# Sliding-window attention with the keys on the partitions, in quarters of TensorE's array, before a mixture of experts

## The chip, the cores and the metric

The kernel runs on one core of a Trainium2 chip. The metric is the device time of one execution in microseconds (us), lower is better. All data are 32-bit floats.

## What is computed

Attention over 8 batches, 8 heads, 576 positions, head dimension 64, with a bias that falls linearly with the distance (slope 2^-(h+1) for head h) and a window of 128 keys that ends at the query. Its rows feed a mixture of 8 experts, of which each row uses the one with the largest gate logit.

```python
scores = scale * np.matmul(q, k.transpose(0, 1, 3, 2))
scores = np.where((rel >= 0) & (rel < 128), scores - slopes * abs(rel), -1e9)
attn = np.exp(scores - scores.max(-1, keepdims=True))
attn = attn / (attn.sum(-1, keepdims=True) + 1e-09)
x = (attn @ v), laid out as (8 * 576, 512)
logits = x @ w_gate                       # (4608, 8)
expert = argmax(logits); gate_w = softmax(logits)[expert]
out = gate_w * (relu(x @ w1[expert]) @ w2[expert])   # 512 -> 1024 -> 512
```

## The kernel before

q and k come with heads and dimensions as rows and batches and positions as columns, so a pair of heads fills the 128 partitions, 64 each. v comes with tokens as rows. The tokens are cut into 36 tiles of 128; nine tiles are two batches.

*Attention* (lines 161 to 245) loops over the tiles. For each of four pairs of heads, the scores `sp` of 128 queries against 256 keys (the tile before and the tile itself) are two products with 64 rows of weights (L183), VectorE scales them and adds the bias (`sn`, L189) and finds the row minimum of the negated scores (`smin`, L198), ScalarE makes the exponentials `pr` and their sums (L201), TensorE transposes them (`pt`, L208), VectorE or ScalarE evicts them (`pT`, L211, L213), and TensorE multiplies them with v (`at`, L217): the transposed probabilities are the weights, 64 columns of v stream. Per tile, VectorE divides by the sums (`x`, L225), TensorE turns the rows (`xt`, L230) for the gate's logits (`lg`, L235), and the row, times its gate weight, is written to `x_rows` in DRAM (L245).

*Routing* (L254 to L343) finds each token's slot and each slot's token, with a one-hot product on TensorE (`tok`, L335). *The experts* (L350 on) gather 128 rows at a time by index (`xg`), turn them (`tp`, L363), multiply with w1 (`hps`, L373) and w2 (`zp`, L386) and scatter the rows to the output (L392). Five tiles per expert are always there, two further tiles are unrolled, and more lie in a loop that these inputs don't enter.

A scheduler orders the instructions of each engine and sets all semaphores. Loads and row writes share SP's DMA queue, indirect ones GpSimd's.

Of the kernel before, what the change touches and what calls it, by code (L numbers as in the profile page):

```python
# [15 lines left out]
P = 128  # L16
MASKED = 1.0e9


@with_exitstack  # L20
def kernel(
    ctx: ExitStack,
    tc: tile.TileContext,
    qT: bass.AP,  # (H*D, B*S), rows (head, dim), columns (batch, position)
    kT: bass.AP,  # the same
    v: bass.AP,  # (B*S, H*D)
    moe_w_gate: bass.AP,  # (Dm, E)
    moe_w1: bass.AP,  # (E, Dm, F)
    moe_w2: bass.AP,  # (E, F, Dm)
    out: bass.AP,  # (B*S, Dm)  # L30
# [27 lines left out]
    consts = ctx.enter_context(tc.tile_pool(name="consts", bufs=1))  # L58
    rte = ctx.enter_context(tc.tile_pool(name="rte", bufs=1))
    w_pool = ctx.enter_context(tc.tile_pool(name="weights", bufs=2))  # L60

    ident = consts.tile([P, P], F32, name="ident")
    make_identity(nc, ident[:])

    # routing constants
    lt_strict = consts.tile([P, P], F32, name="lt_strict")
# [4 lines left out]
    ones_sq = consts.tile([P, P], F32, name="ones_sq")  # L71
    nc.gpsimd.memset(ones_sq[:], 1.0)
    zero_e = consts.tile([P, E], F32, name="zero_e")
    nc.gpsimd.memset(zero_e[:], 0.0)
    keep = consts.tile([P, E, NT], F32, name="keep")
# [3 lines left out]
    def iota(name, shape, pattern, base, mult):  # L79
        t_i = consts.tile(shape, I32, name=name + "_i")  # L80
        t_f = consts.tile(shape, F32, name=name)
# [12 lines left out]
    # the gate's weights, negated: the logits are kept negated  # L94
    wgn = rte.tile([P, DB, E], F32, name="wgn")
# [3 lines left out]
    lgn = rte.tile([P, NT, E], F32, name="lgn")  # L99
    lmin = rte.tile([P, NT], F32, name="lmin")  # L100

    # attention's rows, times their gate weight (positive, so it passes through the expert)
    x_d = nc.dram_tensor("x_rows", (N, Dm), F32, kind="Internal").ap()

    def load_weights(w1_src, w2_src):
        w1 = w_pool.tile([P, DB, F], F32, name="w1")
        w2 = w_pool.tile([P, FB, Dm], F32, name="w2")
# [7 lines left out]
    with tc.tile_pool(name="bias", bufs=1) as b_pool, \  # L115
         tc.tile_pool(name="ld", bufs=3) as ld, \
         tc.tile_pool(name="kld", bufs=2) as kld, \
         tc.tile_pool(name="soft", bufs=4) as soft, \
         tc.tile_pool(name="rows", bufs=2) as rows, \
         tc.tile_pool(name="ps_s", bufs=3, space=PSUM) as ps_s, \  # L120
         tc.tile_pool(name="ps_t", bufs=2, space=PSUM) as ps_t, \
         tc.tile_pool(name="ps_1", bufs=1, space=PSUM) as ps_1:
# [3 lines left out]
        rel_i = b_pool.tile([P, 2 * P], I32, name="rel_i")  # L126
        nc.gpsimd.iota(rel_i[:], pattern=[[-1, 2 * P]], base=P, channel_multiplier=1)
        rel = b_pool.tile([P, 2 * P], F32, name="rel")
        nc.gpsimd.tensor_copy(rel[:], rel_i[:])
        nbias = b_pool.tile([P, H, 2 * P], F32, name="nbias")  # L130
# [6 lines left out]
        nc.gpsimd.affine_select(  # keys 128 or more before the query  # L137
# [11 lines left out]
        def load(c):  # L149
            pair = c * CH // TP  # L150
            if c * CH % TP == 0:
                k_sb[pair] = kld.tile([P, HP, TP * P], F32, name="k_sb")
            q_sb[c] = ld.tile([P, HP, CH * P], F32, name="q_sb")
            v_sb[c] = ld.tile([P, CH, Dm], F32, name="v_sb")
# [6 lines left out]
        for t in range(NT):  # L161
# [9 lines left out]
            c0 = P if j == 0 else 0  # a pair's first tile has no tile before  # L171
            q0 = t % CH * P

            at = ps_1.tile([P, H, D], F32, name="at")
            ssum = rows.tile([P, H], F32, name="ssum")
            # two heads at a time that lie on the same partitions, so that a PSUM bank has one row tile's products
            for g in range(HP):
# [3 lines left out]
                sp = ps_s.tile([P, 2, 2 * P], F32, name="sp")  # L181
# [5 lines left out]
                # the scores, negated  # L187
                sn = soft.tile([P, 2, 2 * P], F32, name="sn")
# [4 lines left out]
                if j == mid:  # the second batch's queries see nothing of the first  # L193
                    nc.vector.memset(sn[HALF:, :, : P + HALF], MASKED)
# [283 lines left out]
```

## Time and profile before

| | |
|---|---|
| median of 2 runs | 1414.22 us (1411.57 to 1416.87) |
| the profiled execution, first to last instruction | 1414.8 us |
| TensorE products busy | 1371.2 us, 97% |
| VectorE, ScalarE, GpSimd busy | 354.4, 294.8, 99.0 us |
| attention's last `lmin` (L237) | at 766.37 us |

The span lies inside the interval of the runs and 0.6 us from their median, so no time of weight lies around it. A busy share is the time in which an engine has an instruction under way; a product that waits for its weights counts as busy. A row of the groups gives the source line, the engine, the operation, the tile written and those read, the shapes, the count, the busy time and the mean duration of one in ns.

### The profile page before, as it was taken

How to read it: one execution, taken by the hardware profiler on the slowest of the kernel's cores; microseconds unless marked ns; L12 is line 12 of the kernel's file. 1: busy time of each engine (PE TensorE's matmuls, PEld its weight loads, DVE VectorE, ACT ScalarE, POOL GpSimd, SP SyncE). 2: the span in 40 equal slices, each digit the busy share in tenths (PEclk: the TensorE clock that was granted, in tenths of full speed). 3: DMA queues.
4: the chain of work that ended last, by engine and by line, in shares of the span. 5: the costliest groups of instructions: out<-in, count | busy, mean ns of one | idle time of the engine just before them, and what ended most of it. 6: DMA issues, size and time to landing. Idle time of an engine off the chain costs nothing.

```text
span 1414.8 us, 12107 instructions
## 1 busy us (share of the span) xinstructions
PE 1371.2 (97%) x4708; PEld 918.1 (65%) x4708; DVE 354.4 (25%) x807; ACT 294.8 (21%) x907; POOL 99.0 (7%) x118
## 2 busy tenths in 40 slices
PE   7999999999999999999996799999999999999996
PEld 5667777777777677776765664647474747474654
DVE  3333333333333433333334410101010101010100
ACT  2322333233333223333322000000000000000000
POOL 2000000000000000000000502020202020101010
PEclk9999999999999999999999999999999999999998
DMA  7422131010211101100000223232323232222221
GB/s 283 142 89 97 38 120 38 28 45 32 83 59 38 53 8 60 38 16 15 8 16 16 83 69 107 78 107 82 108 79 109 76 110 79 80 72 83 78 88 48
DMA packets 45642, 100.96 MB, mean 71 GB/s; under 512 B 3727, under 2 KB 16015, under 8 KB 45584
## 3 DMA queue, kind: packets, MB, share of 16 engines
q1 hardware_dynamic: 38336, 79.70, 16.0%
q0 software_dynamic: 6720, 20.46, 4.2%
q8 instruction: 38, 0.62, 0.2%
q14 instruction: 20, 0.16, 0.0%
q10 hardware_dynamic: 528, 0.02, 0.0%
HBM read 81.28 MB, written 20.45 MB: 72 GB/s over the span
## 4 chain that ended last, share of the span: by engine, by line
PE 54%; issue 38%; POOL 6%; DVE 1%; POOLq 0%; ACT 0%; DVEq 0%; ACTq 0%
PE sp L183 19%; PE at L217 17%; PE pt L208 10%; PE lg L235 4%; POOL out_dram L392 3%; POOL xg L353 3%; PE xt L230 3%; PE tok L335 1%; POOL oh_c L327 0%; POOL nbias L137 0%; POOL nbias L133 0%; POOLq L392 0%; DVE oh_c L323 0%; DVE pre L263 0%; DVE x L225 0%
## 5 line engine op out<-in xcount | busy, mean ns | idle before, releaser
L183 PE MATMUL sp<-k_sb,q_sb 64*128 64x256 f32 (+1 forms) x576 | 290.3, 677 | 10.0 <-DMA k_sb<-in_kT_dram 7.8
L373 PE MATMUL hps<-xgT,w 128*128 128x320 f32 (+1 forms) x1152 | 292.6, 416 | 0.0
L386 PE MATMUL zp<-w,h_sb 128*128 128x512 f32 x672 | 292.4, 592 | 0.0
L217 PEld LDWEIGHTS at<-v_sb,pT 128*128 128x128 f32 x1088 | 243.6, 330 | 50.0 <-ACT pr L201 15.6
L373 PEld LDWEIGHTS hps<-xgT,w 128*128 128x128 f32 x1152 | 209.8, 191 | 84.5 <-issue 5.1
L217 PE MATMUL at<-v_sb,pT 128*128 128x64 f32 x1088 | 258.7, 422 | 1.1 <-ACT pT L213 0.7
L386 PEld LDWEIGHTS zp<-w,h_sb 128*128 128x128 f32 x672 | 125.8, 190 | 149.2 <-issue 149.2
L183 PEld LDWEIGHTS sp<-k_sb,q_sb 64*128 64x128 f32 x576 | 132.6, 312 | 78.6 <-issue 64.8
L208 PE MATMUL pt<-ident,pr 128*128 128x128 f32 x544 | 167.9, 432 | 0.0
L378 DVE TENSOR_SCALAR h_sb<-hps 128x320 f32<-128x320 f32 (+1 forms) x72 | 33.8, 469 | 488.0 <-PE hps L373 486.3
L201 ACT ACTIVATE pr<-sn,smin 128x256 f32<-128x256 f32 (+1 forms) x288 | 139.9, 488 | 66.0 <-DVE lmin L237 30.3
L208 PEld LDWEIGHTS pt<-ident,pr 128*128 128x128 f32 x544 | 104.1, 236 | 69.7 <-issue 52.1
L189 DVE SCALAR_TENSOR_TENSOR sn<-sp,nbias 128x512 f32<-128x512 f32 (+1 forms) x144 | 93.7, 653 | 98.9 <-PE sp L183 93.0
L213 ACT COPY pT<-pt 128x512 f32<-128x512 f32 (+1 forms) x72 | 40.4, 561 | 250.9 <-PE pt L208 250.9
L198 DVE TENSOR_REDUCE smin<-sn 128x2 f32<-128x512 f32 (+1 forms) x144 | 92.5, 645 | 0.4
L380 ACT ACTIVATE h_sb<-hps 128x320 f32<-128x320 f32 (+1 forms) x72 | 30.2, 419 | 298.8 <-PE hps L373 298.8
L391 ACT COPY zo<-zp 128x512 f32<-128x512 f32 x42 | 24.6, 585 | 282.2 <-PE zp L386 256.3
L211 DVE COPY pT<-pt 128x512 f32<-128x512 f32 (+1 forms) x72 | 47.5, 660 | 130.3 <-PE pt L208 130.3
L235 PEld LDWEIGHTS lg<-wgn,xT 128*128 128x128 f32 x288 | 65.3, 331 | 7.6 <-ACT pT L213 6.5
L235 PE MATMUL lg<-wgn,xT 128*128 128x8 f32 x288 | 65.3, 356 | 0.7 <-ACT xT L232 0.7
L327 POOL TENSOR_TENSOR oh_c<-oh_c,tokv 128x639 f32<-128x639 f32 x4 | 9.1, 2265 | 768.5 <-DVE oh_c L323 768.5
L392 POOL DMA_INDIRECT out_dram<-zo,s_idx x42 | 41.6, 990 | 263.9 <-ACT zo L391 249.4
(93 smaller groups left out, 436.8 us busy)
## 6 DMA issues: line engine op xcount, KB each, us to landing
w<-in_moe_w_dram SPq DMA_DIRECT2D x20, 2048.0 KB, 8.9
q_sb<-in_qT_dram SPq DMA_DIRECT2D x12, 768.0 KB, 4.7
k_sb<-in_kT_dram SPq DMA_DIRECT2D x12, 768.0 KB, 7.6
v_sb<-in_v_dram SPq DMA_DIRECT2D x12, 768.0 KB, 4.5
x_rows<-xs SPq DMA_DIRECT2D x36, 256.0 KB, 2.0
xg<-x_rows,g_idx POOLq DMA_INDIRECT x42
out_dram<-zo,s_idx POOLq DMA_INDIRECT x42
wgn<-in_moe_w_gate_dram ACTq DMA_DIRECT2D x1, 16.0 KB, 4.9
```

The source lines that it names most:

```text
L183: nc.tensor.matmul(sp[:, i, c0:], lhsT=q_sb[t // CH][part, h // 2, q0 : q0 + P], rhs=k_sb[pair][part, h // 2, (j - 1) * P + c0 : (j + 1) * ...
L189: nc.vector.scalar_tensor_tensor(sn[:, :, c0:], in0=sp[:, :, c0:], scalar=-(D ** -0.5), in1=nbias4[:, g // 2, :, half, c0:], op0=ALU.mult, ...
L198: nc.vector.tensor_reduce(smin[:], sn[:, :, c0:], axis=AX, op=ALU.min)
L201: nc.scalar.activation(pr[:, i, c0:], sn[:, i, c0:], AF.Exp, bias=smin[:, i : i + 1], scale=-1.0, accum_out=ssum[:, h : h + 1],)
L208: nc.tensor.transpose(pt[:, i, kb, :], pr[:, i, kb * P : (kb + 1) * P], ident[:])
L211: nc.vector.tensor_copy(pT[:, :, c0 // P :, :], pt[:, :, c0 // P :, :])
L217: nc.tensor.matmul(at[:, h, :], lhsT=pT[:, i, kb, :], rhs=v_sb[kt // CH][:, kt % CH, h * D : (h + 1) * D], start=(kb == c0 // P), stop=(kb ...
L230: nc.tensor.transpose(xt[:, db, :], xf[:, db * P : (db + 1) * P], ident[:])
L235: nc.tensor.matmul(lg[:], lhsT=xT[:, db, :], rhs=wgn[:, db, :], start=(db == 0), stop=(db == DB - 1))
L373: nc.tensor.matmul(hps[:, :step], lhsT=g["w"][0][:, db, fb * P : (fb + 1) * P], rhs=g["xT"][:, db, c : c + step], start=(db == 0), stop=(d ...
L386: nc.tensor.matmul(zp[:], lhsT=g["h"][:, fb, j * P : (j + 1) * P], rhs=g["w"][1][:, fb, :], start=(fb == 0), stop=(fb == FB - 1),)
L392: ins = nc.gpsimd.indirect_dma_start(out=out[:, :], out_offset=bass.IndirectOffsetOnAxis(ap=g["si"](j), axis=0), in_=zo[:], in_offset=None ...
```

## The change

The attention stage is written anew; the experts keep their code.

- A unit is two batches (`bp`) and two heads (`hp`), 16 in all. Scores are made transposed: 64 keys on the partitions, up to 192 queries on the columns. The two heads lie on the two halves of the array's rows, the two batches on the two halves of its columns, so four products use one quarter (64 x 64) each. `GR` packs nine key blocks (block, first column, queries) into four groups of `GC` = 384 columns; `KB` is 64 keys. The loop has 64 groups and makes scores two groups (`AHEAD`) before they are used.
- ScalarE takes the exponential of the scores without a shift, VectorE multiplies by `fac`, the exponential of bias and mask, which is made once. The result is already in the layout of the product with v, so nothing is transposed; v's blocks are the weights, also in quarters.
- The sums over keys are products on TensorE with a matrix of zeros and ones (`ind`), 32 columns of the array each, so four lie beside each other.
- Gate logits are made from rows that are not yet divided (`gate`, again in strips of 32 columns), turned (`turn`), divided and turned into gate weights per pair of batches (`scale`); `row` turns a tile of x and multiplies by both factors at the eviction. These steps are put behind the next units' work by a list (`tasks`), of which `some` does the next entry: three for the gate, `turn` and `scale`, then five for nine rows.
- The attention's instructions are kept in the order written (`tc.manual_schedule()`).
- Each sum is checked to lie in 1e-18 to 1e24; a flag goes through DRAM, and if it is set at the end, the kernel of before (`general_path`) runs and overwrites the output.
- Expert 0's weights are loaded during attention, expert 1's no longer; the routing's constants are made after attention instead of at the start.

```diff
+        GR = [[(0, 0, 192), (1, 192, 192)], [(2, 0, 192), (3, 192, 192)], [(4, 0, 192), (5, 192, 192)],
+              [(6, 0, 192), (7, 192, 128), (8, 320, 64)]]
+        QH = [(0, 5 * KB), (5 * KB, 4 * KB)]
...
+            qk = pool("qk", 3)
+            ep = pool("ep", 5)
+            ps_s = pool("ps_s", 2, space=PSUM)
+            ps_a = pool("ps_a", 1, space=PSUM)
+            ps_m = pool("ps_m", 2, space=PSUM)
...
+            for h in range(H):
+                sl = -(2.0 ** (-8.0 * (h + 1) / H))
+                for c0, n in ((0, 192), (192, 128), (320, 64)):
+                    nc.scalar.activation(fac[:, h, c0 : c0 + n], rel[:, :n], AF.Exp, scale=sl)
...
+            def scores(i):
+                u, g = divmod(i, 4)
+                sp = ps_s.tile([P, 2, 512], F32, name="sp")
+                for kb, c0, n in GR[g]:
+                    for c in range(2):
+                        for r in range(2):
+                            hs = slice(r * D, (r + 1) * D)
+                            nc.tensor.matmul(
+                                sp[c * KB : (c + 1) * KB, r, c0 : c0 + n],
+                                lhsT=k_sb[u][hs, c, kb * KB : (kb + 1) * KB],
+                                rhs=q_sb[u][hs, c, kb * KB : kb * KB + n], start=True, stop=True,
+                            )
+                pe = ep.tile([P, 2, GC], F32, name="pe")
+                nc.scalar.activation(pe[:], sp[:, :, :GC], AF.Exp, scale=SCALE)
...
+                    nc.vector.tensor_tensor(pe[:], pe[:], fac[:, h0 : h0 + 2, :], op=ALU.mult)
...
+            def values(u, half, kbs):
...
+                for kb in kbs:
+                    pe, c0, n = block(u, kb)
+                    lo, hi = max(q0, kb * KB), min(q0 + qn, kb * KB + n)
+                    for c in range(2):
+                        for r in range(2):
+                            nc.tensor.matmul(
+                                acc[r * D : (r + 1) * D, c, lo - q0 : hi - q0],
+                                lhsT=v_sb[bp][c * KB : (c + 1) * KB, kb, (2 * hp + r) * D : (2 * hp + r + 1) * D],
+                                rhs=pe[c * KB : (c + 1) * KB, r, c0 + lo - kb * KB : c0 + hi - kb * KB],
+                                start=(c, r) not in begun, stop=True, skip_group_check=True,
+                            )
...
+            def finish(u, half):
...
+                nc.scalar.copy(xT[bp][:, hp, : 2 * LQ].rearrange("p (b q) -> p b q", b=2)[:, :, q0 : q0 + n], acc[:, :, :n])
...
+                for par, lo, hi, pe, off in ops:
+                    for r in range(2):
+                        j = 2 * r + par
+                        nc.tensor.matmul(
+                            sm[32 * j : 32 * j + 32, lo - q0 : hi - q0],
+                            lhsT=none[:] if pe is None else ind[:, hp, :],
+                            rhs=fac[:, 0, :KB] if pe is None else pe[:, r, off + lo : off + hi],
+                            start=j not in begun, stop=True, skip_group_check=True,
+                        )
...
+            def gate(bp, c):
...
+                c0, n = ((0, LQ), (LQ, LQ), (2 * LQ, P))[c]
+                for hp in range(HP):
+                    nc.tensor.matmul(
+                        ps[32 * hp : 32 * hp + 32, :n], lhsT=wgd[:, hp, :], rhs=xT[bp][:, hp, c0 : c0 + n],
+                        start=True, stop=True,
+                    )
...
+            def row(bp, t):
+                ps = ps_m.tile([P, 512], F32, name="m")
+                for hp in range(HP):
+                    nc.tensor.transpose(ps[:, hp * P : (hp + 1) * P], xT[bp][:, hp, t * P : (t + 1) * P], ident[:])
+                xs = rows.tile([P, H, D], F32, name="xs")
+                nc.vector.tensor_tensor(
+                    xs[:], ps[:].rearrange("p (h d) -> p h d", h=H),
+                    rsg[bp][:, t, :].unsqueeze(2).to_broadcast([P, H, D]), op=ALU.mult,
+                )
...
+            for i in range(NG):
+                u, g = divmod(i, 4)
...
+                if i + AHEAD < NG:
+                    scores(i + AHEAD)
+                if g == 0:
+                    values(u, 0, (0, 1))
+                elif g == 1:
+                    values(u, 0, (2, 3))
+                elif g == 2:
+                    values(u, 0, (4,))
+                    finish(u, 0)
+                    some()
+                    values(u, 1, (3, 4, 5))
+                else:
+                    values(u, 1, (6, 7, 8))
+                    finish(u, 1)
+                    some()
+                    if hp == HP - 1:
+                        tasks.extend(behind(bp))
...
+        fl = fp.tile([1, 1], I32, name="fl")
+        nc.sync.dma_start(fl[:], flag_d[:, 0:1])
+        wrong = nc.values_load(fl[0:1, 0:1], min_val=0, max_val=1)
+    with tc.If(wrong > 0):
+        general_path(tc, qT, kT, v, moe_w_gate, moe_w1, moe_w2, out, S, H)
```

## Rows read from the trace of the kernel before

**Rows 1.** The page: busy us and share; the granted clock in 40 slices, in tenths.
```profile
PE 1371.2 (97%) x4708; PEld 918.1 (65%) x4708; DVE 354.4 (25%) x807; ACT 294.8 (21%) x907; POOL 99.0 (7%) x118
...
PEclk9999999999999999999999999999999999999998
```

**Rows 2.** Stretches: us, busy (count) of each engine, granted clock, DMA share, GB/s.
```profile
0.00:30.00 30.00, 20.00 (x66) 13.13 (x66) 12.18 (x31) 8.08 (x29) 8.03 (x30) 1.00 0.94 333
...
150.00:700.00 550.00, 550.00 (x1930) 397.70 (x1929) 198.53 (x475) 175.36 (x582) 0.00 (x0) 1.00 0.13 44
```

**Rows 3.** Attention's TensorE groups by form, whole run: busy us, mean ns.
```profile
L183 PE MATMUL sp<-k_sb,q_sb 64*128 64x256 f32 x512 | 273.5, 703 | 0.0
L217 PE MATMUL at<-v_sb,pT 128*128 128x64 f32 x1088 | 258.7, 422 | 1.1 <-ACT pT L213 0.7 <-DVE gw L241 0.4
...
L208 PE MATMUL pt<-ident,pr 128*128 128x128 f32 x544 | 167.9, 432 | 0.0
```

**Rows 4.** Timeline, 300 to 322 us: start, length, merged instructions, idle before.
```profile
306.25 2.08 PE L183 MATMUL sp<-k_sb,q_sb 64*128 64x256 f32 x6
...
313.35 2.07 PE L183 MATMUL sp<-k_sb,q_sb 64*128 64x256 f32 x4
...
317.68 0.50 PEld L183 LDWEIGHTS sp<-k_sb,q_sb 64*128 64x128 f32 x2 [0.33 <-issue]
317.68 1.22 PE L183 MATMUL sp<-k_sb,q_sb 64*128 64x256 f32 x2
```

**Rows 5.** Same shapes early and late: transposes by timeline, L373 by stretches.
```profile
308.26 1.11 PE L230 MATMUL xt<-ident,x 128*128 128x128 f32 x4
...
1382.19 0.60 PE L363 MATMUL tp<-ident,xg 128*128 128x128 f32 x4
...
807.95:810.06 2.11, 2.11 (x5) 1.36 (x6) 1.00 0.75 206
810.06:812.17 2.11, 2.11 (x9) 1.52 (x8) 1.00 0.72 223
```

**Rows 6.** The experts' products: groups by form, then the timeline at 1375 us.
```profile
L386 PE MATMUL zp<-w,h_sb 128*128 128x512 f32 x672 | 292.4, 592 | 0.0
L373 PE MATMUL hps<-xgT,w 128*128 128x320 f32 x1024 | 278.0, 433 | 0.0
...
1375.05 7.31 PE L373 MATMUL hps<-xgT,w 128*128 128x128 f32 x64
```

**Rows 7.** ScalarE's and VectorE's groups by form.
```profile
L201 ACT ACTIVATE pr<-sn,smin 128x256 f32<-128x256 f32 x256 | 127.4, 500 | 53.6 <-DVE lmin L237 30.3 <-DVE rsum L222 16.7 <-DVE smin L198 5.6
...
L189 DVE SCALAR_TENSOR_TENSOR sn<-sp,nbias 128x512 f32<-128x512 f32 x128 | 87.0, 682 | 83.3 <-PE sp L183 82.0 <-ACT pr L201 1.3
...
L213 ACT COPY pT<-pt 128x512 f32<-128x512 f32 x64 | 37.5, 585 | 236.5 <-PE pt L208 236.5
...
L225 DVE TENSOR_TENSOR x<-at,rsum 128x512 f32<-128x512 f32 x36 | 24.9, 692 | 108.9 <-PE at L217 108.9
...
L201 ACT ACTIVATE pr<-sn,smin 128x128 f32<-128x128 f32 x32 | 12.5, 392 | 12.4 <-DVE smin L198 12.4
...
L189 DVE SCALAR_TENSOR_TENSOR sn<-sp,nbias 128x256 f32<-128x256 f32 x16 | 6.6, 420 | 15.6 <-PE sp L183 10.9 <-POOL nbias L137 4.1 <-ACT pr L201 0.6
...
L213 ACT COPY pT<-pt 128x256 f32<-128x256 f32 x8 | 2.9, 364 | 14.4 <-PE pt L208 14.4
...
L82 POOL IOTA tokv_i<- 128x36 int32 x1 | 0.2, 153 | 0.0
```

**Rows 8.** The page: the instruction queue's packets and MB; a small load's landing.
```profile
q8 instruction: 38, 0.62, 0.2%
...
wgn<-in_moe_w_gate_dram ACTq DMA_DIRECT2D x1, 16.0 KB, 4.9
```

**Rows 9.** Timeline: the last tile's `lmin`, and the first `oh_c` of the routing.
```profile
766.37 0.16 DVE L237 TENSOR_REDUCE lmin<-lgn 128x1 f32<-128x8 f32 x1
...
776.74 0.82 DVE L323 TENSOR_TENSOR oh_c<-iota_r,rc 128x639 f32<-128x639 f32 x1
```

More of the change, by code (lines that the diff above doesn't have):

```diff
@@ L20, with general_path @@
 @with_exitstack
-def kernel(
+def general_path(
     ctx: ExitStack,
@@ L56 @@
     assert LC <= 512
[L58 to L62, printed above, removed]
+    consts = ctx.enter_context(tc.tile_pool(name="g_consts", bufs=1))
+    rte = ctx.enter_context(tc.tile_pool(name="g_rte", bufs=1))
+    w_pool = ctx.enter_context(tc.tile_pool(name="g_weights", bufs=2))
+    ident = consts.tile([P, P], F32, name="g_ident")
     make_identity(nc, ident[:])
-    lt_strict = consts.tile([P, P], F32, name="lt_strict")
+    lt_strict = consts.tile([P, P], F32, name="g_lt_strict")
     nc.gpsimd.memset(lt_strict[:], 1.0)
@@ L79, in iota @@
     def iota(name, shape, pattern, base, mult):
-        t_i = consts.tile(shape, I32, name=name + "_i")
-        t_f = consts.tile(shape, F32, name=name)
+        t_i = consts.tile(shape, I32, name="g_" + name + "_i")
+        t_f = consts.tile(shape, F32, name="g_" + name)
         nc.gpsimd.iota(t_i[:], pattern=pattern, base=base, channel_multiplier=mult)
@@ L112 @@
     expert_w = {}
[L115 to L126, printed above, removed]
+    with tc.tile_pool(name="g_bias", bufs=1) as b_pool, \
+         tc.tile_pool(name="g_ld", bufs=3) as ld, \
+         tc.tile_pool(name="g_kld", bufs=2) as kld, \
+         tc.tile_pool(name="g_soft", bufs=4) as soft, \
+         tc.tile_pool(name="g_rows", bufs=2) as rows, \
+         tc.tile_pool(name="g_ps_s", bufs=3, space=PSUM) as ps_s, \
+         tc.tile_pool(name="g_ps_t", bufs=2, space=PSUM) as ps_t, \
+         tc.tile_pool(name="g_ps_1", bufs=1, space=PSUM) as ps_1:
+        rel_i = b_pool.tile([P, 2 * P], I32, name="g_rel_i")
         nc.gpsimd.iota(rel_i[:], pattern=[[-1, 2 * P]], base=P, channel_multiplier=1)
-        rel = b_pool.tile([P, 2 * P], F32, name="rel")
+        rel = b_pool.tile([P, 2 * P], F32, name="g_rel")
         nc.gpsimd.tensor_copy(rel[:], rel_i[:])
-        nbias = b_pool.tile([P, H, 2 * P], F32, name="nbias")
+        nbias = b_pool.tile([P, H, 2 * P], F32, name="g_nbias")
         for h in range(H):
@@ L151, in load @@
             if c * CH % TP == 0:
-                k_sb[pair] = kld.tile([P, HP, TP * P], F32, name="k_sb")
-            q_sb[c] = ld.tile([P, HP, CH * P], F32, name="q_sb")
-            v_sb[c] = ld.tile([P, CH, Dm], F32, name="v_sb")
+                k_sb[pair] = kld.tile([P, HP, TP * P], F32, name="g_k_sb")
+            q_sb[c] = ld.tile([P, HP, CH * P], F32, name="g_q_sb")
+            v_sb[c] = ld.tile([P, CH, Dm], F32, name="g_v_sb")
             cols = slice(c * CH * P, (c + 1) * CH * P)
@@ L172 @@
             q0 = t % CH * P
-            at = ps_1.tile([P, H, D], F32, name="at")
-            ssum = rows.tile([P, H], F32, name="ssum")
+            at = ps_1.tile([P, H, D], F32, name="g_at")
+            ssum = rows.tile([P, H], F32, name="g_ssum")
             for g in range(HP):
@@ L186 @@
                     )
-                sn = soft.tile([P, 2, 2 * P], F32, name="sn")
+                sn = soft.tile([P, 2, 2 * P], F32, name="g_sn")
                 nc.vector.scalar_tensor_tensor(
@@ L204 @@
                     )
-                pt = ps_t.tile([P, 2, 2, P], F32, name="pt")
+                pt = ps_t.tile([P, 2, 2, P], F32, name="g_pt")
                 for i in range(2):
@@ L237 @@
             nc.vector.tensor_reduce(lmin[:, t : t + 1], lgn[:, t, :], axis=AX, op=ALU.min)
-            gex = rows.tile([P, E], F32, name="gex")
-            gw = rows.tile([P, 1], F32, name="gw")
+            gex = rows.tile([P, E], F32, name="g_gex")
+            gw = rows.tile([P, 1], F32, name="g_gw")
             nc.scalar.activation(gex[:], lgn[:, t, :], AF.Exp, bias=lmin[:, t : t + 1], scale=-1.0, accum_out=gw[:])
@@ L261 @@
         )
-        pre = sm.tile([P, E, NT], F32, name="pre")
+        pre = sm.tile([P, E, NT], F32, name="g_pre")
         nc.vector.tensor_tensor_scan(
@@ L291 @@
         )
-        xe_f = sm.tile([1, NX + 1], F32, name="xe_f")
+        xe_f = sm.tile([1, NX + 1], F32, name="g_xe_f")
         nc.vector.reduce_sum(xe_f[:, :NX], xk[:], axis=AX)
@@ L366, in layer1 @@
     def layer1(g):
-        g["h"] = wk_pool.tile([P, FB, NJ * P], F32, name="h_sb")
+        g["h"] = wk_pool.tile([P, FB, NJ * P], F32, name="g_h_sb")
         step = min(LC, g["n"] * P)
@@ L383, in layer2 @@
         for j in range(g["n"]):
-            zp = mps.tile([P, Dm], F32, name="zp")
+            zp = mps.tile([P, Dm], F32, name="g_zp")
             for fb in range(FB):
@@ L397, in layer2 @@
             if g["apart"]:
-                tc.declare_no_dep(ins, group="rows_out", reason="disjoint rows")
-                tc.add_to_no_dep_group("rows_out", ins)
+                tc.declare_no_dep(ins, group="g_rows_out", reason="disjoint rows")
+                tc.add_to_no_dep_group("g_rows_out", ins)
     def fetch(ex):
```

596 lines of the change are left out of this document (543 added, 53 removed).

## The prediction

> **What bounds the kernel now.** I read the page's busy shares first, then the stretches, then the groups by form, and last the order of single instructions. TensorE is busy 97% of the span [rows 1]. In the steady part of attention it is busy all of the 550 us, VectorE 199 and ScalarE 175 [rows 2]: attention is bound by TensorE, and what the other engines do is hidden. Attention ends at 766.4 us with the last tile's `lmin` [rows 9]; 648.4 us of the span of 1414.8 lie behind it (routing, experts, end). The median of the runs, 1414.2, is that span to within 0.6, so sums against the span need no correction.
>
> The groups say where those 766 us go [rows 3]: one scores product a head (273 us in the full form), 1088 weight loads and products against `v` (259), 544 transposes of the probabilities (168). Each f32 product is two instructions, a transpose one. The reader is to see that `at` streams only 64 columns for 128 loaded weights, and that the scores use 64 of the 128 rows.
>
> Two things decide what the same arithmetic costs in another shape. First, halves of the array do run together: four score instructions take 2.07 us, but six that lie on both halves take 2.08, where two take 1.22 [rows 4]. From four against two, one 256-column instruction costs (2.07 - 1.22) / 2 = 0.425 us: 1.66 ns a column. Second, the clock. Four 128x128 transposes take 1.11 us in attention and 0.60 in the last experts; the first 2.11 us of the first expert hold 5 products, the next 2.11 hold 9 [rows 5]. Full-speed products cost 292.4 / 672 = 0.435 us for 512 columns [rows 6]: 0.85 ns a column, half of 1.66. The granted clock reads full speed in both [rows 1]; against it I go by the durations: attention runs at the 1.2 GHz level throughout, the experts at 2.4.
>
> **The change part by part.** It removes the 544 probability transposes, their 144 evictions, the maxima and accumulator reads. A unit is two batches by two heads; there are 16. Its TensorE work, in columns times instructions:
> - scores: (7 x 192 + 128 + 64) = 1536 columns on each of four quarters, two instructions each: 12,288. At 1.66 ns 20.4 us one after another, 5.1 if four run at once;
> - values: the same 1536 columns a quarter, over 11 pieces: 20.4 or 5.1;
> - sums, moved from ScalarE's accumulator to TensorE: (2 x 1536 + 128) x 2 = 6,400: 10.6, or 2.7 with four strips of 32 columns at once;
> - gate, per pair of batches 4 x 1152 x 2 = 9,216: 15.3 or 3.8, a quarter of it per unit: 3.8 or 1.0;
> - 45 transposes per pair of batches at 0.213 us (128 columns at 1.66): 9.6, per unit 2.4;
> - changes of the array's shape, about six a unit: the scores' weight loads sat 0.33 us behind such a change [rows 4]. 2 us; ends 0 (overlapped) and 4.
>
> With all four quarters at once a unit is 5.1 + 5.1 + 2.7 + 1.0 + 2.4 + 2 = 18.3 us at the low level and about half, 9.2, at the high one; with no overlap 20.4 + 20.4 + 10.6 + 3.8 + 2.4 + 1 = 58.6 at the low one. Before, 766 / 16 = 48. Rows 4 show two row halves at once; column halves and strips they do not show, so the overlap lies between 1 and 4. I take 4: the two halves seen cost nothing extra, which is as near as a row comes.
>
> The other engines, per unit. ScalarE: four exponentials of 768 elements, 0.81 us by the copies' slope (585 against 364 ns for 512 and 256) or 0.93 by the exponentials' [rows 7], 3.5; evictions of 640, 384 and 128 elements 0.70 + 0.48 + 0.25; `turn` 0.36: 5.3. VectorE: four multiplies of 768 at 682 + 256 x 1.02 = 0.94 [rows 7], 3.8; two sums 0.49 + 0.42; per pair of batches the gate's adds 1.7, some 30 small operations of `scale` 6.3, nine rows at 0.69 = 6.2, a quarter of it 3.6: 8.3. So at the low clock TensorE has 18.3 against 8.3 and hides them; at the high clock 9.2 against 8.3, and nothing hides a wait: the multiply of two groups ahead queues on VectorE behind `scale`, whose operations wait for `turn`'s copies. Between 9.2 (perfect) and 17.5 (the two added up) I take 12, nearer the first as the loop runs two groups ahead. Loads: 1.18 MB of q and k, 0.59 of v, 0.59 of rows per unit; the first 30 us moved 333 GB/s [rows 2], so 7.1 us a unit: hidden, and the floor if all else shrinks. `x_rows` and loads share SP's queue, and a row's write waits for its multiply there; loads queued behind it are for two units later, so it holds nothing.
>
> The start: ScalarE makes `fac` in 24 exponentials of 64 to 192 columns ahead of the first real one. By the exponentials' slope they take about 0.25 to 0.3 each once the accumulator is gone, 7 us after some 3 of set-up: 10 us until TensorE can go on. The end: the last pair's gate, `scale` and nine rows have nothing left to hide them: 1.7 + 6.3 + 6.2 of VectorE, with transposes and copies between, 20 us (ends 14 and 30).
>
> Behind attention: first, GpSimd builds the constants after attention, 40 small iotas among them, some 10 us by its 0.15 us operations [rows 7], beside VectorE's 10 us from `lmin` to `oh_c` [rows 9]: 0 to 8, I take 3. Second, expert 1's weights, loaded during attention before, now load beside expert 0's gathers: 0 to 5, I take 3; they are wanted only an expert later. Third, the flag's load and branch at the end: a small load lands in 4.9 us [rows 8] and no work is left to cover it: 0 to 12, I take 5. Together +11. The experts' products don't change.
>
> **Sum.** At the high level: 10 + 16 x 12 + 8 (four times 2 us of `scale` in the way) + 20 = 230; 230 + 648.4 + 11 = 889 us. Against the span of 1414.8 a saving of 525.
>
> **A rule against the change.** In rows 6, products on the same rows come 0.27 us apart for 320 columns, which is the streaming alone: the next weights load under the running product. The Trainium skill ("TensorE: Matmul & The Clock Gate", section on packing small matmuls) says a weight load overlaps a running product only when its row group differs; rows 6 disagree, as all their products use all rows. If it held between column halves, the 160 score and value instructions a unit would each show their load: rival 3's 965 us by the rule, 889 by the rows.
>
> **The rivals.**
> 1. The clock stays at the low level, as in all of attention before, although TensorE never paused there. For it: the durations of rows 4 and 5 there; against it: the first expert's dense products raised it at once [rows 5], and the change takes out the short products and most transposes. 10 + 16 x 18.3 + 25 + 659 = 987. Two quarters at once with the high level gives about the same, since both halve the rate.
> 2. Only the row halves overlap, at the low level: 10.2 + 10.2 + 10.6 + 3.8 + 2.4 + 2 = 39 us a unit, 624 + 35 + 659 = 1318; with strips overlapping by two, 32 a unit and 1206.
> 3. Weight loads between column halves show: 64 weights are half of the 128 whose load sets `at`'s pace of 259 / 1088 = 0.238 [rows 3], so 0.12 us, 160 of them over two row halves 9.5 us a unit, halved at the high level: 889 + 76 = 965. This is the skill's rule above.
> 4. TensorE cannot be fed: 225 pairs of load and product a unit. The densest stretch shows 64 in 7.31 us, 0.114 each [rows 6], but it is set by its 128 columns. At that pace 25.7 us a unit: 411 + 35 + 659 = 1105. Against it: in rows 4, six came in the time of four. The instruction queue carried 0.62 MB in 38 packets over the whole run [rows 8]; attention's 3604 pairs alone now want three quarters of that in a fifth of the time.
> 5. Slower: the quarters don't overlap at all (a wait between tiles of one bank or shape): 58.6 x 16 + 35 + 659 = 1632. It decides below an overlap of about 1.4, where a unit costs 45 us.
> 6. The check fails and `general_path` runs behind it: 889 + 1414 = 2303. The row sums of weights near 1 in a window lie between 1 and 128, far inside 1e-18 to 1e24, so under 1%.
>
> **How the numbers follow.** Forecast (four at once, high level) 0.55; rivals 1 and 3, with a clock that changes between levels, 0.25 together; rival 4 0.05; rival 2 0.07; rivals 5 and 6 0.03; better than 840, down to loads' floor 10 + 16 x 7.1 + 20 + 659 = 803, 0.05. The forecast's own bounds: 840 (10 us a unit, small end terms) to 950 (15 a unit, large ones). The range takes in rivals 1 and 3 with it: 840 to 1020, about 0.8. Faster by over 2% (what a measurement of this kernel can tell) 0.96, within 2% 0.01, slower 0.03.
>
> **What would show it.** After: TensorE's instructions of `sp` four to a start time, a unit in 12 us, attention ending near 230; transposes of the rows at 0.105 us pitch (else rival 1); starts of the second column half held back to the end of the first (rivals 2, 3); TensorE idle with no releaser (rival 4). The forecast is wrong if VectorE's multiply turns out to be what TensorE waits for most, at over 14 us a unit, or if the clock falls back in the waits.

## The result and the profile after

The changed kernel takes 875.65 us, median of two runs (874.09 to 877.21), against 1414.22: a ratio of 0.619, 95% interval 0.6145 to 0.6229. Forecast were 889, with 840 to 1020 as the range. The profiled execution is the one of 877.21 us; its span is 875.4. Of the six executions of the version with both repairs below, one took 3822 us and the others 862 to 866; its median is over all six.

The page of the changed kernel: busy us and share, the granted clock in 40 slices, the instruction queue, and attention's groups with the idle time ahead of them (these rows answer to [rows 1, 3, 8]).
```profile
PE 790.2 (90%) x5674; PEld 510.1 (58%) x5674; DVE 207.1 (24%) x421; ACT 137.3 (16%) x267; POOL 97.7 (11%) x166
...
PEclk8899999988559999999999999999999999999997
...
q8 instruction: 47, 0.77, 0.4%
...
L654 PE MATMUL at<-pe,v_sb 64*64 64x192 f32 (+2 forms) x1408 | 65.1, 297 | 16.4 <-DVE pe L628 7.8
...
L619 PE MATMUL sp<-q_sb,k_sb 64*64 64x192 f32 (+2 forms) x1152 | 63.1, 338 | 8.4 <-DMA q_sb<-in_qT_dram 7.5
...
L625 ACT ACTIVATE pe<-sp 128x768 f32<-128x768 f32 x64 | 51.8, 810 | 97.1 <-PE sp L619 95.6
L628 DVE TENSOR_TENSOR pe<-pe,fac 128x768 f32<-128x768 f32 x48 | 45.9, 957 | 54.3 <-ACT pe L625 54.3
```
`sp` and `at` are now busy for 128 us where `sp`, `at` and the transposes took 700 [rows 3]. By the forecast's own count each streams 12,288 columns a unit: one after another at the high clock (0.85 ns a column, [rows 6]) 10.4 us a unit, 167 us each in all. The mean of one instruction (297 and 338 ns) says nothing here, since several run at once; the busy time of the group does.

The timeline shows the order of four groups in the steady part, TensorE alone (start, length, merged instructions).
```profile
119.16 0.83 PE L654 MATMUL at<-pe,v_sb 64*64 64x192 f32 x16
...
119.81 0.84 PE L619 MATMUL sp<-q_sb,k_sb 64*64 64x192 f32 x24
...
120.46 0.73 PE L654 MATMUL at<-pe,v_sb 64*64 64x192 f32 x16
...
121.01 0.83 PE L619 MATMUL sp<-q_sb,k_sb 64*64 64x192 f32 x16
```
The 24 instructions at 119.81 are three key blocks of 192, 128 and 64 columns, each on four quarters in two instructions: 384 x 8 = 3072 columns. One after another they would take 2.6 us; the next group starts 0.65 us later. That is the factor of four.

Now the stretches: one undisturbed unit, then a unit in which the gate's `scale` runs, cut in two (columns as in [rows 2]).
```profile
53.30:61.30 8.00, 7.51 (x218) 6.67 (x215) 3.98 (x6) 4.38 (x8) 0.00 (x0) 1.00 0.30 104
...
121.90:129.90 8.00, 6.00 (x129) 4.99 (x125) 6.59 (x27) 2.73 (x5) 0.00 (x0) 1.00 0.11 25
129.90:138.30 8.40, 5.54 (x104) 4.52 (x108) 4.89 (x12) 3.13 (x7) 0.00 (x0) 0.80 0.40 131
```
An undisturbed unit takes 8.0 us with TensorE busy 94%; this one holds scores, values and sums only, as the first pair's gate and rows come later. (For the unit's borders the start of every fourth exponential L625 is taken.) The unit with `scale` takes 16.4, TensorE is busy 11.5 of it, and the granted clock leaves 1.00 in the second half. What stands in the way is read from the timeline there:
```profile
125.47 0.65 DVE L740 TENSOR_TENSOR s<-gsr 128x8 f32<-128x8 f32 x6 [0.98 <-ACT gsr L730]
...
128.51 1.18 DVE L761 TENSOR_REDUCE logits<-pr 128x72 f32<-128x576 f32 x1
...
130.25 0.26 ACT L767 ACTIVATE ex<-ex 128x72 f32<-128x72 f32 x1 [4.64 <-DVE ex L764]
...
130.42 0.79 ACT L625 ACTIVATE pe<-sp 128x768 f32<-128x768 f32 x1
...
131.42 0.95 DVE L628 TENSOR_TENSOR pe<-pe,fac 128x768 f32<-128x768 f32 x1
...
132.28 0.42 DVE L698 TENSOR_TENSOR sumT<-m,sumT 128x256 f32<-128x256 f32 x1
...
132.76 1.11 PE L781 MATMUL m<-ident,xT 128*128 128x128 f32 x4 [4.13 <-DVE sumT L698]
```
TensorE stops for 4.13 us, and its row names what ended the stop: `sumT` (L698), which empties one of the two buffers `m`. It stands in VectorE's queue behind the whole chain of `scale`, which ends at 131.5, and behind the multiply of the next scores (L628). ScalarE's queue is held too: the gate's exponential `ex` (L767) stands in it ahead of the next scores' exponential (L625) and waits 4.64 us for the same chain. But that exponential is done at 131.21, before VectorE is free, so in this stop VectorE's chain comes last. The four transposes after it take 1.11 us, the low-clock figure of [rows 5]; at 87.94 us the same four take 0.66.

Another wait shows in the list of waits for 32 to 200 us (total us, times, the longest):
```profile
DVE xs L783 <- DMA x_rows<-xs: 14.3, 5, 5.5
```
VectorE's multiply of a row waits until an earlier row has been written out of its buffer.

The end of attention and the routing, by the timeline (they answer to [rows 9]), then the end of the span:
```profile
216.29 0.23 DVE L762 TENSOR_REDUCE lmax<-logits 128x9 f32<-128x72 f32 x1
...
229.57 0.82 DVE L974 TENSOR_TENSOR oh_c<-iota_r,rc 128x639 f32<-128x639 f32 x1
...
250.21 1.19 POOL L1007 DMA_INDIRECT xg<-x_rows,g_idx  x1 [7.13 <-DVE s_idx L996]
...
262.14 0.77 PE L1027 MATMUL hps<-xgT,w 128*128 128x320 f32 x2
...
858.67 0.30 SPq L1109 DMA_DIRECT2D fl<-flag  x1
859.45 0.98 POOL L1046 DMA_INDIRECT out_dram<-zo,s_idx  x1 [13.03 <-ACTq L1094]
```
Attention's gate ends at 216.3 where it ended at 766.4. From there to the end of the span are 659.1 us, before 648.4. The routing runs at the low level, as slices 11 and 12 of the clock row show: the granted clock is 0.50 from 214.4 us for 47.8 us.

### The profile page after: what moved, and what is told of

The parts are those of the page before. It is cut to its first block, busy times and chain, and to the rows that moved or that the text cites. A ratio compares the mean times of both kernels' runs of the same rounds, so it can differ in the third digit from the quotient of the medians.

```text
span 875.4 us, 12886 instructions
## 1 busy us (share of the span) xinstructions
PE 790.2 (90%) x5674; PEld 510.1 (58%) x5674; DVE 207.1 (24%) x421; ACT 137.3 (16%) x267; POOL 97.7 (11%) x166
## 4 chain that ended last, share of the span: by engine, by line
issue 62%; PE 13%; POOL 8%; DVE 6%; DMA 6%; ACT 1%; SPq 1%; POOLq 0%; DVEq 0%; ACTq 0%
POOL out_dram L1046 5%; PE sp L619 4%; POOL xg L1007 4%; PE at L654 4%; DMA x_rows<-xs 3%; PE tok L986 2%; DMA v_sb<-in_v_dram 2%; PE m L687 2%; PE m L707 1%; DMA xg<-x_rows,g_idx 1%; PE m L781 1%; DVE xs L783 1%; ACT pe L625 1%; DVE pe L628 1%; DVE pr L754 1%
## 5 line engine op out<-in xcount | busy, mean ns | idle before, releaser
L654 PE MATMUL at<-pe,v_sb 64*64 64x192 f32 (+2 forms) x1408 | 65.1, 297 | 16.4 <-DVE pe L628 7.8
L619 PE MATMUL sp<-q_sb,k_sb 64*64 64x192 f32 (+2 forms) x1152 | 63.1, 338 | 8.4 <-DMA q_sb<-in_qT_dram 7.5
L1007 POOL DMA_INDIRECT xg<-x_rows,g_idx x42 | 40.3, 960 | 271.5 <-PE tp L1017 254.3
L625 ACT ACTIVATE pe<-sp 128x768 f32<-128x768 f32 x64 | 51.8, 810 | 97.1 <-PE sp L619 95.6
L654 PEld LDWEIGHTS at<-pe,v_sb 64*64 64x64 f32 x1408 | 49.7, 142 | 27.9 <-DVE pe L628 9.4
L628 DVE TENSOR_TENSOR pe<-pe,fac 128x768 f32<-128x768 f32 x48 | 45.9, 957 | 54.3 <-ACT pe L625 54.3
L619 PEld LDWEIGHTS sp<-q_sb,k_sb 64*64 64x64 f32 x1152 | 45.8, 146 | 15.9 <-DMA k_sb<-in_kT_dram 4.5
L781 PE MATMUL m<-ident,xT 128*128 128x128 f32 x144 | 27.4, 327 | 20.8 <-DVE sumT L698 16.8
L1018 DVE COPY xgT<-tp 128x512 f32<-128x512 f32 x42 | 27.7, 688 | 53.4 <-PE tp L1017 53.4
L687 PE MATMUL m<-pe,ind 128*32 128x192 f32 (+2 forms) x704 | 30.9, 294 | 1.7 <-issue 1.7
L783 DVE TENSOR_TENSOR xs<-m,rsg 128x512 f32<-128x512 f32 x36 | 24.5, 685 | 17.3 <-DMA x_rows<-xs 14.3
```

Of the source, the lines that this page charges most:

```text
L619: nc.tensor.matmul(sp[c * KB : (c + 1) * KB, r, c0 : c0 + n], lhsT=k_sb[u][hs, c, kb * KB : (kb + 1) * KB], rhs=q_sb[u][hs, c, kb * KB : k ...
L625: nc.scalar.activation(pe[:], sp[:, :, :GC], AF.Exp, scale=SCALE)
L628: nc.vector.tensor_tensor(pe.rearrange("p r (k c) -> p r k c", k=2), pe.rearrange("p r (k c) -> p r k c", k=2), fac[:, h0 : h0 + 2, None, ...
L654: nc.tensor.matmul(acc[r * D : (r + 1) * D, c, lo - q0 : hi - q0], lhsT=v_sb[bp][c * KB : (c + 1) * KB, kb, (2 * hp + r) * D : (2 * hp + r ...
L687: nc.tensor.matmul(sm[32 * j : 32 * j + 32, lo - q0 : hi - q0], lhsT=none[:] if pe is None else ind[:, hp, :], rhs=fac[:, 0, :KB] if pe is ...
L781: nc.tensor.transpose(ps[:, hp * P : (hp + 1) * P], xT[bp][:, hp, t * P : (t + 1) * P], ident[:])
```

## The experiments

Where a run gave an interval, it stands against runs of the kernel before on the same chip, all with medians of 1416 to 1417 us. First theory: the time hangs on four quarters running together. Its rival: TensorE is near enough to waiting for other engines that the order matters little. Three kernels change the order of the products alone.

**Batches in turn, heads in turn, one quarter at a time.** In `scores` and `values` (one shown; the second kernel has `r` outermost and `c` innermost, the third `c`, `r`, then `kb`):
```
-                for kb, c0, n in GR[g]:
-                    for c in range(2):
+                for c in range(2):
+                    for kb, c0, n in GR[g]:
                         for r in range(2):
```


> The changed kernel with the batch as the outer loop of the score and value products, so that only the two row halves (two heads) stand side by side in the queue. All work stays. If the gain comes from four quarters at once: the score and value products of a unit (12,288 columns times instructions each, 0.845 ns) need 10.4 us in place of 5.2, so the bare unit goes from 8.0 to 13.2 us; 16 x 5.2 = 83 us more, less what now hides the present waits (4.3 us a unit): 915 to 960 us, the clock still high. If column halves did not run together in the changed kernel (rival 2), nothing changes: 876. If half the array does not keep the clock up (rival 1), a unit is 26 us and the whole near 1100.

> The same with the head as the outer loop, so that only the two column halves (two batches) stand side by side on the same rows. Four quarters theory: the same 915 to 960 us as with the batches in turn. If the weight loads of two column halves on the same rows show (rival 3), 0.06 us for each of 160 instructions a unit comes on top of that, up to 80 us more: 1000 to 1040.

> The same with batch and head as outer loops, so that one quarter works at a time: the price of rival 5. Four quarters theory at the high clock: 20.8 us for scores and values, a bare unit of 23.6, 16 x (23.6 - 12.3) = 181 more: near 1060. If a quarter of the array alone does not keep the clock up: 47 us a unit, near 1430, as slow as the kernel before. If the order in the queue makes no difference: 876.

Measured: 879.59 us (ratio 0.6209, 0.6197 to 0.6222), 879.28 (0.6207, 0.6195 to 0.622) and 894.09 (0.6312, 0.6291 to 0.6333). The losses that the theory forecast (915 to 960 twice, near 1060) did not come: even with one quarter at a time the kernel loses some 18 us, and the other two can't be told from the changed kernel. The first time is near the 876 that was written down for "column halves did not run together", so the time alone does not refute rival 2; the bursts below do. The page of the third shows why:
```profile
L654 PE MATMUL at<-pe,v_sb 64*64 64x192 f32 (+2 forms) x1408 | 100.5, 300 | 6.7 <-DMA v_sb<-in_v_dram 2.9
...
L619 PE MATMUL sp<-q_sb,k_sb 64*64 64x192 f32 (+2 forms) x1152 | 93.3, 340 | 7.6 <-DMA q_sb<-in_qT_dram 7.6
```
Both groups are busy for longer, but an undisturbed unit takes 10.1 us, where its scores and values one after another would take 2 x 10.4 alone: they still overlap, though each quarter's products are issued together. Its timeline from 28 us:
```profile
28.55 0.90 PE L619 MATMUL sp<-q_sb,k_sb 64*64 64x192 f32 x16
...
29.90 1.74 PE L619 MATMUL sp<-q_sb,k_sb 64*64 64x192 f32 x21
```
The 16 instructions at 28.55 stand in the program as four for each quarter in turn. One quarter's four need 0.65 us (4 x 192 x 0.85 ns), so one quarter after the other would take 2.6; all 16 take 0.90, hardly more than the 0.83 of the changed kernel. Products that stand twelve instructions apart must have run together. The next group, at 29.90, does not manage it as well (1.74 us). So the order within a group counts for little. The undisturbed unit grew from 8.0 only to 9.0, 9.0 and 10.1 us in the three kernels. Neither theory is right as it stood: the quarters do run together, and it isn't the program's order that makes them.

**Four more buffers for rows.** The wait for `x_rows` is taken away by buffers.
```
-            rows = pool("rows", 2)
+            rows = pool("rows", 6)
```


> The changed kernel with six buffers in place of two for the rows xs that are written to x_rows. VectorE waited 14.3 us for these writes between 32 and 200 us. Theory: the waits delay the multiplies of the scores and with them TensorE, and the low clock after them costs more: 10 to 20 us less, 855 to 866. Rival: VectorE has slack (8.3 of 12.3 us a unit), so at most the 3 us that TensorE loses nearby: 872 to 877.

874.96 us (871.15 to 876.98 in four runs; ratio 0.6168, 0.6151 to 0.6185): no difference from the changed kernel's that can be told, as the rival had it. The waits for the writes were gone, and the two units that took 14.3 and 15.0 us with them (from 107.6 and 159.5 us in the profile after) took 9.3 and 10.1 (11.9 and 10.5 in a second profile of the changed kernel, so the wait is not always as long); but the units with `scale` still took 17.1 to 17.5, and the early units, in which the loads still land, were some 5 us slower in this profile. Attention's gate ended at 212.6 us, against 216.3 and, in that second profile, 210.8, so the wait's price lies within what one execution differs from the next.

**TensorE alone.** All of the computation is left out; bursts of the shapes in question run back to back, with dense products between them.
```
+        for i in range(32):              # four quarters; the others fix r, c or both
+            c, r = i // 2 % 2, i % 2
+            nc.tensor.matmul(acc[half(c), r, :192], lhsT=w[half(r), :64], rhs=a[half(r), :192], ...)
```


> TensorE alone: the whole computation is left out, the output holds nothing of the reference. Dense full-array products of 512 columns lie between the bursts and raise the clock. Bursts of 32 products (64 instructions) of 192 columns, 0.162 us each at the high clock: in one quarter 10.4 us; two row halves in turn 5.2; two column halves in turn 5.2 (if weight loads of column halves on the same rows show, 8 or more); four quarters 2.6; one strip of 32 columns 10.4; four strips 2.6. Then long runs of the forms of the kernel before: 256 instructions of 128 weights and 64 columns, 200 transposes, 80 instructions of 256 columns on half the rows. Theory (low clock in attention because of these forms): the granted clock falls in each of the three, which take 55, 43 and 34 us. Rival (the clock stays low there because of the waits and the shape changes between them): it stays high, 27, 21 and 17 us. Last, 640 instructions in four quarters (26 us, high clock by both) and 160 in one quarter (26 us if a quarter keeps the clock, 52 if not).

Its timeline, one row a burst (32 products, 64 instructions in the first six):
```profile
26.43 10.61 PE L54 MATMUL acc<-a,w 64*64 64x192 f32 x64
...
47.47 5.42 PE L58 MATMUL acc<-a,w 64*64 64x192 f32 x64
...
63.32 5.42 PE L62 MATMUL acc<-a,w 64*64 64x192 f32 x64
...
79.16 2.83 PE L66 MATMUL acc<-a,w 64*64 64x192 f32 x64
...
92.42 10.59 PE L69 MATMUL strip<-a,w 128*32 128x192 f32 x64
...
113.43 2.81 PE L73 MATMUL strip<-a,w 128*32 128x192 f32 x64
...
126.58 28.69 PE L77 MATMUL turned<-a,w 128*128 128x64 f32 x256
...
165.46 22.00 PE L80 MATMUL turned<-ident,a 128*128 128x128 f32 x200
...
197.69 17.53 PE L83 MATMUL acc<-a,w 64*128 64x256 f32 x80
...
225.65 26.23 PE L87 MATMUL acc<-a,w 64*64 64x192 f32 x640
...
262.31 26.21 PE L90 MATMUL acc<-a,w 64*64 64x192 f32 x160
```
One quarter 10.61 us, two row halves 5.42, two column halves 5.42, four quarters 2.83; one strip of 32 columns 10.59, four strips 2.81. Streaming alone is 64 x 192 x 0.85 ns = 10.4 us for one quarter, so the weight loads show nowhere, between column halves no more than between row halves. Second, the short forms of the kernel before, 128 weights for 64 columns (0.112 us each, in attention 0.238 [rows 3]), transposes (0.11) and products on half the rows (0.219), ran at the high clock for 29, 22 and 18 us, and so did the last two, in four quarters and in one (26 us each). So none of these forms lowers the clock within that time when it is high already. Whether one would do so later, or would raise a low clock, these bursts don't show: dense products lie ahead of each.

**No flag.** The range check's flag, the load of it and the general path behind it are left out.

> The changed kernel without the flag's write and read and without the branch to the general path: sums out of range would go unnoticed. The end behind the last scatter goes from 15.9 us back to the 10.2 of the kernel before: 5 to 6 us less, 869 to 871. If the range check costs something inside (a wider product, code loading), more than that.

865.54 us (863.92 to 867.17), beside 872.35 (870.05 to 877.96 in four runs) for the changed kernel measured with it: 6.8 less. From the last scatter to the end of the span it is 862.2 - 851.5 = 10.7 us where it was 875.4 - 859.5 = 15.9.

**`scale` cut in two.** Its second half, from the gate's exponential on, goes one step later; rows move up.
```
-                    [lambda: [turn(bp, k) for k in range(3)], lambda: scale(bp)],
-                    [lambda: row(bp, 0), lambda: row(bp, 1)], ...
+                    [lambda: [turn(bp, k) for k in range(3)]], [lambda: scale(bp)],
+                    [lambda: weight(bp), lambda: row(bp, 0), lambda: row(bp, 1)],
+                    [lambda: row(bp, 2), lambda: row(bp, 3)], [lambda: row(bp, k) for k in (4, 5, 6)], ...
```


> The changed kernel with the second half of scale (the gate's exponential and what follows it) as a task of its own, half a unit later, and turn in one before it. Theory: ScalarE's queue held the next scores' exponential behind the gate's, which waits for VectorE's whole chain; TensorE stood still 4 us a pair of batches, and the clock fell after it. Three such stops in the loop, each with 3 to 7 us at the low clock: the unit of 17 us becomes 12 or less, 860 to 866 us. Rival: VectorE's chain itself holds the multiplies, wherever the exponential stands: 872 to 877.

> The changed kernel again, as the measure for the small differences beside it: 874 to 877.

879.31 us (876.57 to 884.41 in four runs) against 872.35 (870.05 to 877.96 in four): not faster. The unit with `scale` fell from 16.4 to 11.2 us (the split shortens the chain in both queues and puts a step between `turn` and `scale`, so it does not say which of them the gain comes from), and another rose to 18.1, where the timeline shows the step of three rows:
```profile
106.30 0.69 DVE L789 TENSOR_TENSOR xs<-m,rsg 128x512 f32<-128x512 f32 x1 [6.01 <-DMA x_rows<-xs]
...
107.05 2.32 PE L787 MATMUL m<-ident,xT 128*128 128x128 f32 x8 [3.97 <-DVE xs L789]
```
The write to `x_rows`, whose removal alone gained nothing that could be told, now stops VectorE for 6 us and TensorE for 4.

**Both together.** If the write takes `scale`'s place as the wait that stops the unit, the cut `scale` and six row buffers together must gain what neither did.

> The split of scale and six row buffers at once. With the split alone the long unit moved from scale to the step with three rows, where VectorE waited 6.0 us for a write of xs to land behind the loads; with the buffers alone scale's stop stayed. Theory: two waits that stand in for each other, so only both gone show a gain: no unit over 13 us, three stops of 5 to 7 us less, 855 to 863. Rival: the loads set the pace of a pair of batches (4 units in some 48 us), 870 to 876.

863.23 us, ratio 0.6099, 0.6089 to 0.611: below the changed kernel's 0.6145 to 0.6229 and below the run with six buffers alone. Its stretch from 97.8 to 149.0, and after it the same stretch of the changed kernel:
```profile
97.80:149.00 51.20, 45.82 (x1062) 38.02 (x1065) 34.99 (x72) 21.24 (x36) 0.00 (x0) 1.00 0.75 220
```
```profile
97.80:149.00 51.20, 41.53 (x901) 33.08 (x893) 29.94 (x65) 19.06 (x32) 0.00 (x0) 0.93 0.62 180
```
1062 matmuls in place of 901, and a clock that does not fall. The units with `scale` take 11.1 to 11.9 us, and attention's gate ends at 198.2 in place of 210.8 or 216.3. This version beats both kernels.

**The kernel before with dense products in it.** How much of the gain is the clock? Into attention of the kernel before come full-width products whose results are unused: first 12 ahead of four of the tiles, then 6 ahead of every second tile.
```
+            if t % 2 == 0 and t > 0:          # first run: if t in (2, 11, 20, 29), 12 products
+                dense = ps_1.tile([P, 512], F32, name="lg")
+                for _ in range(6):
+                    nc.tensor.matmul(dense[:], lhsT=ident[:], rhs=nbias[:, 0:2, :]..., start=True, stop=True)
```


> The kernel before with four bursts of 12 dense products (128 x 128 weights, 512 columns) ahead of tiles 2, 11, 20 and 29; their results are not used. A burst costs 10 us at the high clock, up to 20 at the low one. The long runs of the burst kernel kept the high clock through each form of this attention. Theory A (the level that attention is in holds until a long stop: it starts low, for the early loads, and nothing in it is dense enough to raise it): after the first burst the clock stays high, TensorE's 20.9 us a tile becomes 11 to 14, where VectorE's and ScalarE's chains begin to show: 1414 - 34 x 7 to 9 + 50 = 1160 to 1230 us. Theory B (the mixture, with its shape changes, brings the clock down again whatever it was): 1414 + 50 = 1440 to 1470, and the change's clock comes from its denser products.

> The kernel before with six dense products ahead of every second tile, 17 bursts of 5 to 10 us. With four bursts the clock rose each time, fell again after 17 to 68 us although TensorE did not stop, and a tile took 13.3 to 15.1 us in place of 21 while it was up. Theory: bursts this near keep it up most of the time; 36 tiles at 14 and 17 bursts at 5: attention 590 in place of 766, 1235 us, up to 1290 if the clock is up for two thirds of it. So about half of what the change takes from attention would be the clock, half the quarters. Rival: the clock falls right after each short burst: 17 x 10 on top of 1414 less what little it gives, 1500.

The first took 1384.7 us (1362.66 and 1406.73), with these stretches:
```profile
249.00:296.80 47.80, 47.70 (x263) 32.31 (x261) 25.54 (x60) 18.94 (x61) 0.00 (x0) 1.00 0.12 45
296.80:419.70 122.90, 122.90 (x425) 89.21 (x425) 42.14 (x104) 41.12 (x137) 0.00 (x0) 0.50 0.17 60
419.70:487.90 68.20, 68.10 (x403) 48.29 (x402) 39.83 (x91) 32.71 (x106) 0.00 (x0) 1.00 0.15 51
487.90:573.30 85.40, 85.40 (x286) 60.11 (x285) 27.70 (x72) 27.36 (x94) 0.00 (x0) 0.50 0.10 34
```
Neither theory's time came out (1160 to 1230, 1440 to 1470). The bursts start at 56.5, 246.7, 416.5 and 569.0 us and end 12 to 13 us later. In each the clock rises to 1.00, and it stays there for 17 to 68 us, the rest of the burst included; then it falls with TensorE busy all the time. It also rose twice with no burst near, from 98.8 to 102.2 and from 699.6 to 706.4 us. The second took 1223.16 us (1205.57 to 1241.7), 193 less than the kernel before beside it, with 102 more products. Its groups, to be held against [rows 3]:
```profile
L193 PE MATMUL sp<-k_sb,q_sb 64*128 64x256 f32 x512 | 162.5, 464 | 0.0
...
L227 PE MATMUL at<-v_sb,pT 128*128 128x64 f32 x1088 | 158.7, 295 | 1.5 <-ACT pT L223 0.7 <-DVE pT L221 0.2
```
The same scores take 162.5 us in place of 273.5, the same values 158.7 in place of 258.7. The theory's 1235 was near, its rival's 1500 far off. Of the unchanged kernel beside these runs single executions took 1377.79 and 1381.34 us, so its clock may rise now and then without any burst; no trace of those is kept.

## Why the prediction was right, and where not

**Four at once: right.** The step that carried the sum, an overlap of four taken from two row halves [rows 4], is what the bursts measured: 10.61 against 2.83 us. Rivals 2 and 5 fall with it, rival 4 with 24 instructions in 0.65 us. The instruction queue carried 0.77 MB; from 32 to 200 us TensorE's longer waits without a releaser, the sign of rival 4, add up to 5.3 us.

**Weight loads between column halves: right, against the rule.** Rival 3 is refuted: 5.42 us for column halves as for row halves, and one quarter alone is at its streaming time. The Trainium skill ("TensorE: Matmul & The Clock Gate", section "Part 3: Packing small matmuls — row/col tiling") has the loads overlap only where the row group differs; by the measurement they overlap also where the rows are the same. The same section lets a load go ahead into a background weight buffer as well; that sentence agrees with these bursts, the "only" does not.

**The unit: 12.25 for 12, in part by luck.** The first exponential starts at 9.68 us (10 forecast), and the last product of `at` at 205.7: (205.7 - 9.7) / 16 = 12.25. The sum had 12 + 0.5 a unit. TensorE's work was sized well: 9.2 forecast, of which a unit without gate and transposes makes 7.5, and 8.0 measured for such a unit. From 50 to 200 us TensorE is busy 121.7 of 150 us, which is 9.9 of a 12.25 us unit with the spells at the low clock in it. The mechanism named for the stops is the one seen: VectorE's work queues behind `scale` (the text named the multiply, the trace shows `sumT` behind it). Their size was not: the three units with `scale` take 16.4 to 17.4 us, over 8 more than a bare one, where 2 were added, and the clock is lower behind the stop. And two waits that the text put at nothing took time. The rows' writes are the next point. The loads, "hidden", held the start of the loop:
```profile
18.08 0.69 PE L654 MATMUL at<-pe,v_sb 64*64 64x128 f32 x4 [3.58 <-DMA v_sb<-in_v_dram]
...
30.00:50.00 20.00, 15.09 (x360) 13.22 (x360) 7.81 (x11) 7.64 (x13) 0.00 (x0) 0.91 0.81 211
```
The first four units, which have no gate and no rows in them, took 43.6 us in place of 32. Against sixteen bare units (128 us) the loop's 196 us hold 12 more in these four, 26 in the three with `scale`, 13 in two that wait for `x_rows`, and 17 in the rest, where gate and rows are. The 12 were chosen between 9.2 and 17.5; that they cover waits which the text did not have is chance.

**`x_rows`: wrong.** "So it holds nothing" looked at the loads behind the row's write in SP's queue, and not at the buffer that the write holds. VectorE waits 14.3 us for it between 32 and 200 us. Alone its price could not be told from run to run. With `scale` cut in two it is what stops the unit, and with both repairs the time falls to 863.2, 9 and 12 us below the changed kernel's two medians: it is the next wait in line.

**The clock: right level, reason not shown.** The text gave the missing short products and transposes as what would let the clock rise. The bursts show these forms running at the high level for up to 29 us, but not what they do to a low one. What the runs do show: the mixture of the kernel before starts at the low level and stays there for long stretches, 146.8 us in one; in the run with four bursts each burst raised it, it rose twice without one, and it fell again each time before attention ended. In the changed kernel the granted clock in attention is high but for short spells, each in or just behind a stop of TensorE such as the 4.13 us ahead of 132.76; then it is low through the routing, from the stop of 6.9 us ahead of 219.84 on. A clock that falls back in the waits was one of the text's own signs of being wrong; it did fall back, and the time came out near the forecast even so. Why the mixture of the kernel before loses the level without a stop stays open, and with it why the new one keeps it.

**How much is the clock, as an estimate.** In the run with 17 bursts attention ended at 554.7 us; a burst is 12 instructions of 0.435 us, 5.2, so 89 in all. Without them some 466, mostly at the high clock: of the 550 us that attention lost, about 300 would be the clock and 250 quarters and left-out work. Some 70 us of that attention still ran at the low level (two stretches of 100 us show a granted clock of 0.85), so the clock's part is rather more than less; and the profile is that of the fastest of the four runs. Clock and shapes were changed together here, so the split is worked out, not measured, and what the quarters and the left-out work each give was not tried apart.

**Tail and what lies behind: right in sum.** The tail was 10 us, not 20, because the last rows were written beside the routing; the routing's start paid for some of it: from the gate's end to the first gather 33.9 us, before 31.2. The flag was forecast at 5; its removal gave 6.8 by the medians, and the end of the trace is 5.2 shorter. Everything behind attention came to 659.1 for 659.4.

Sum against sum: 10 + 16 x 12.25 + 10.6 + 659.1 = 875.7 for 889; the 13 us lie in the tail (10) and the units (4, `scale`'s 8 counted in).

## What to carry to other kernels

Where an f32 product uses 64 rows and 64 columns of TensorE, put four independent ones on the four quarters; in this kernel their exact order mattered little (875 to 894 us). When a stop is found, look for the next wait on the same engines before judging a repair: here two repairs gained nothing that could be told alone, and 9 to 12 us together. Before crediting a new layout with a gain, check by the duration of a known shape which clock the old one ran at.

## What the hardware showed beyond that

- The profile's clock row starts from the first event recorded. In the kernel before it reads 9 in all of attention [rows 1] while the durations are those of the low level [rows 5]; a score instruction has a mean of 703 ns there, and 705 in a stretch of the run with four bursts that reads 0.50. So a 9 ahead of the first event tells nothing.
- By its durations TensorE stayed at the low level in the kernel before while busy all the time, 550 of 550 us [rows 2], and 102 unused dense products made that kernel 193 us faster.
- Products of different quarters overlap although the program issues one quarter after the other: 16 instructions in 0.90 us where one quarter after the other would take 2.6 (28.55 us in the run with one quarter at a time).
